# A Conformer block on one core: the small gate's halves trade partitions, small operations take their engine from a table, and the written-out orders are replaced

## The chip, the cores and the metric

The kernel runs on one core of one Trainium2 chip. Its time is the device time of one execution in microseconds, here the median of several runs. The core has four engines that compute, each with its own in-order queue: PE (matrix products into PSUM), ACT (activation functions, copies), DVE (elementwise work, statistics) and POOL (GpSimd, elementwise work without PSUM). SP's queue issues most DMAs. Engines wait for one another by semaphores. A queue never passes a waiting instruction, so the order in which instructions stand on an engine is part of the kernel.

## The reference

Two sequences of 4000 tokens, 144 channels, 4 heads of 36, a depthwise convolution of 5 taps; inputs and output are bf16.

```python
def reference(x, w_ff1a, w_ff1b, w_qkv, w_o, w_pw1, dw, w_pw2, w_ff2a, w_ff2b):
    h = _layernorm(x, axis=-1)
    h = _silu(h @ w_ff1a) @ w_ff1b
    x = x + 0.5 * h
    h = _layernorm(x, axis=-1)
    qkv = h @ w_qkv
    ...
    p = _softmax(scores, axis=-1)
    att = jnp.einsum('bhqk,bhkd->bhqd', p, v)
    ...
    x = x + att @ w_o
    h = _layernorm(x, axis=-1)
    h = h @ w_pw1
    a, b = (h[..., :D].copy(), h[..., D:].copy())
    h = a * _sigmoid(b)
    ...
    for i in range(K):
        c = c + hp[:, i:i + T, :] * dw[i][None, None, :]
    x = x + _silu(c) @ w_pw2
    h = _layernorm(x, axis=-1)
    h = _silu(h @ w_ff2a) @ w_ff2b
    x = x + 0.5 * h
    return _layernorm(x, axis=-1)
```

## The kernel before

The 8000 tokens are cut into 16 chunks of 500 (four blocks of 125 tokens), eight per sequence. Each chunk goes through the first feed-forward part and the projections (`pre`), then the attention of its 500 queries against the 4000 keys of its sequence, then what follows attention: the output projection (`post1`), the gated product (`glu`, `glu_left`), the convolution, the second feed-forward part and the last normalisation (`post2`). The parts before and after are spread between the tiles of attention of other chunks.

**Attention.** Keys come in tiles of 64, 62 per sequence and a rest of 32; 16 chunks times 63 give 1008 tiles in a fixed sequence. A tile takes four score matmuls (two heads at a time in two PSUM banks, 128x1000 values). For a tile of type A one ACT instruction takes the exponential of both banks into a slot of `PT`. For type D DVE makes it without ACT: two conversions of 128x500 to int16, a bit operation, a product and a second bit operation on 128x1000 (`ymw_args`); type W does both conversions in one instruction. R is the rest tile. A tile of type A needs four value matmuls, one of type D or W eight, since its exponential is a sum of two parts. Values gather in PSUM banks 6 and 7, and `epilogue` takes them out when a chunk is complete.

**The gated product.** Of the 144 channels, 128 go through `glu`. The other 16 of all four blocks are packed side by side by `glu_left`: the matmuls against the padded weights `WPZ` leave the value half in PSUM partitions 0 to 63 and the gate half in 64 to 127. ACT's tanh (the sigmoid is made from it) reads partitions 64 to 127 and writes `TH` on 0 to 63; a DVE instruction multiplies that with the value half. It runs once per chunk, 16 times.

**Small operations.** `copy` takes projections and transposes out of PSUM (`KT`, `QT`, `VA`, `XTB`, `XTQ`), on ACT or DVE. `residual` adds a product to `X`: ten or fewer matmuls for two blocks into one bank, then a DVE instruction that scales PSUM, adds `X` and writes `X`. `ln` makes a normalisation: statistics on DVE, then on one engine the variance plus epsilon (`RS` from `ST`), on POOL its reciprocal root (an exponent of -0.5), then the normalised rows `XN`, on POOL in the middle of the kernel, on DVE or ACT in the first chunks and at the end.

**What sets the order.** A planner runs the program once with costs and makes instructions in an order of its own, which also fixes what depends on what. Six tables then replace its choices. `TYPES` gives each tile its type; `BANKS` and `SLOTS` its PSUM banks and its slots of `PT`; `PLACES` the banks of all other PSUM tiles. `settle` builds the attention instructions anew from these. `ORDER` holds for each engine the order of all steps in two characters each; `Rec.arrange` sorts by it and derives the waits for PSUM banks and slots. `Rec.replay` then issues all instructions, so that most rows of the profile have its line, L546; instructions are told apart by the names of their tiles.

Of the kernel before, what the change touches and what calls it, by code (L numbers as in the profile page):

```python
# [13 lines left out]
H = 4  # L14
# [26 lines left out]
        '+V+U+?*z*{+4+I+<+O+M+N+Z+Y+2#-+^+_+1+P+F+b+E+c+D+3+C+J+f+m+l#.+p+q+W+e+d+X+u+t+`+]+g+[+n+o+x+y#/+}+|'
        '#0,,,+,$+a+v+T+S,0,/+w+s+z,!,%,4,3#1,8,7,.+r+j+k+{,1,B,A,<,;+Q+R,#+h,F,E,5,2,-,6,:,I,J+i,M,9,N,C,D#2'
        ',U,R,Q,(,&,*,),K,V,],[#3,`,a,S,P,=,@,d,e#4,h,i,T,l,G,H,>,?,r,s#5,v,w,L,O,m,j,z,{#6-#-!,k,f,b,c,g-&-.'
        '--#7-2-1,X,W,t-(,y,x-6-5-$-%,u-9,},|-:#8,Z-3-=->-4-7-A-8-F,Y-B-E-/-;-0-+-<-K-L-)-,-*-?-O-P-S-T,n-@,o'
        ',^-Z-Y,_-D,p,q-C-^-_#;#9-c-b#:#=#>#<-g-f-J-`-]-[-d-k-j-e-r-a-R-I-o-n#?#@-s-G-X-h-H-W-x-y#A#C#B-|-}-Q'
        '-z-l-i.%.$-{-M.--U-q.).*#D.3.4-N-p...!-m.7.8#E.;.<.@.+.(.5-V.?.##F.6.D.C.=.G-w.&.H.:.9.,-v-u.B.K.L.R'
        '.>.F.S.E.Y.X-t.J.2.].^./.O.0.e.N.M.b.a.I.t.f.1.A.Q.P#G#H.s.p.o.V.[.`.T.W.Z.d.i.x.w#I.u.h.g.j.|.{._.v'
        '.c.r.U.z.y/$/#/(///.#J/2/3/)/!/%/&.q/7/6#K/;/:#L.n/D/>/E/4/0/-/</1/H/=/I.}/?.m/5/8#M/M/L/,/9/*/Q/P/G'
        '#N/X/Y/O/N/F/+/B/K/U/T#O/_/S/i/h/l/C/p/m/J.l#P/q/R/A/Z/^/@/c/b/{/z/a/`/]0!0#/t/[/V.k/W0.0-#Q020&01/k'
        '060%0$050(/j/o0//}/u/|0@0?0409/s/n030D0C00#R0H0G/r08070:/f/g0K0L#S0P0O#T/d/e0S0T0A0E0F0_0M0N0^0B0+0,'  # L50
        '0W0)0g0c0b0R0I0J0Q0V0U0f0X#U0k0j0=0*0d0`0a0n0o#W0s0r0>#V#X0w0v0<0l0z0{0q0u0p0]/x0m0t0;/y1)1*0[0y0e1!'
        '1.1-#Y12110i1+0x1,0h1#1615#Z1:19#[1=1>#]1;1B1E1A1<17181%1$1(1K1&1L1F/w130|0}1O1P#^#_1S1T1@1?1C1X1I1N'
        '1D1Q1R1[1J1W1b1c1U0Z141M/v1]1/0Y1V1f1g#`1q1p1G1H1j101u1t#a1y1x1k1h1d1e1_1`2(2&1v1a1Z1|1^1i2,2+1{1z#b'
        '2/201Y1}2*1w2)292:231n1s2=2>1r#c211o2B2A2-242.2L2K2?2@1l2;2!2F2O2P2<1m2%2E2S2T#d2X2Q2W222M2N2#252R2U'
        '2]2[2$26#e282g2Z2C2`2V2a2h2Y#f2d2I2n2m2y2J2^2D2b2c2q2r2_2G2z2e2f2u2v2H273#3$#i#h3)3(2k2t3-3,#g30312w'
        '2x3&2}2l2o34352s3+2j3*3=3<39382i333!3%2p323B3C37363.3/3F3G#j3K3J2|3N2{3A3:3;3U3T3O3@3X3Y3M3D3a#k3^3]'
        '3E3L3>3h3S3g3Q3H3I3V3[3R3b3k3l3`3P#l3o3?3_3p3i3j3y3z3f3m3W3s3Z4!3n3}#m4&4%3q3t41403r4*4$3{3c3|4544#n'
        '49483d3e424+4#434=4<#o4@4A#p4E4D#q#r4H4I3w473x464L4M#t#s4V4W4/4.4,4)4(4K4[4Z#u4`4_4C4P4;4B4-4:4j4i4F'
        '4Q3u4G4d4n4m3v4b4c4a4Y4r4q4X4^4J4l4?4]4v4u#w#v5#4U4>5$4p5)4w4x4T4O5(4S4y4N4R4h5-5,4z4k#x51505+545&4s'
        '5.5/5:5;4e554g5*4f5?5>4o53524t5B5C5=5L#y5M4{5%5A4}4|5F5!5Q5P59565E5D#z5U5T5N5<575G5@5X5Y#{5^5]#|5b5a'  # L60
        '5S585W5V5f5Z5[5e5R5i5w5_5s5r5d5c5O5J5I5H5K5l5`5g5h5v5j5k5{5z#}5m6!6#5x5t5y6.6&$!6-5}6(5|6%616$62$#66'
        '65$$6364$%676:695u5p6>6/606=686+$&6H6G6A5q6<6K6L$(6B6I6O6*6P6@6)6Y6Z6?6;5o6S6N6,$)$*6M6_6]6^6c5n6b6J'
        '6E6R6Q6F6T6[$+6f6a6m6`6l6D6C6e6q6p6d6g$,6t6u$-6x6y$.6V6|7$6o6}6U6X6r$/7%7+7,6W6{6n706v6s6z6k7/736w7#'
        '796j7:7!$0746h7>7=7*7)6i717A7B$17E7F$27J7I7.7;$3727Q7N7M7-7($4757R7W7X7<7&767C7]7K7[7L78777@7f7P7?7H'
        '7O7g7`$57j7k7G7Z7U7a7Y7D7o7n$67y7x7i7^7_7h7r7T7}7|$77V8$8%7z7s7S7l7{8*8)$884838(8-7e7d8#8&8887$97q7p'
        '8!8.8;8<$:8?8@7b7m7t867u8C8>8I8J8=$;8M8N8+8D7v7c8K8,8Q8R898:8A8B$<8]8[7w8U8P85808/8a8`$=8e8d8V8S8_8O'
        '8H8G8c8h8i8b$>$?8m8l8g8f8p8T8^8L8j8k818z8y9!8}8o8E828s8F8n8X8W8Z8Y8q8r9&9%9+8t9*$@9.94958|9)989$9#8{'
        '99$A9=9<96979,9-9G8w9/9F9($B9K9J9>9;8x9@9O9N$C9S9R9:9A8u9I8v9W9V9L9?9M9H9Z9a9b$D9f9e9[909U92939T9j9i'
        '9Q$E9s9t9g9Y9h9P919m9x9w9d9c$F9|9{9n9C:*9X:+9B9z9^9u9v9`:#:/:.$G:29l9_:3:$:-9k:!9q9r:6:0:7:,9]9E:::1'
        ':A:@$H:4:;:8:E9y:D:(9p:):H9D9}:I:L9o:5:S:R$I:M:F:%:W:&:V:B:[:U:J:G:Z:_:?:9:C:e:f$J:=:<:j:i:`:X:Q:T:g'  # L70
        ':^:m:n:>:h:K:]:q:Y:w:x$K:{:|:r:o:P;#;$$L;/;.:a:O:y:d:p;2;3:c:N;6:z;(;7;!;0$M;1:}:t;@:s;A;E;:;&:u:v;D'
        ';%:k:l;);H;I;4:b;B;;;5;M;L$N$O;8;P;J;Q;U;N;,;O;9;T;F;C;+;*$P;_;G;X;`;-;K;>;c;S;=;d;R;Y;?;V$Q;h;g;<;W'
        ';l;k$R;w;o;p;e;f;i;j;^;];t;s$S;b;z;n;q;{<)<*<$;m<%$T$U<3<4;y;x<8<-<7<.;a;r;v;u;Z<<<;;[$V<?<@$W$X$Y$Z'
        '$[<C<D<,<5<H<&<(<9<:<+<G<2;|<0</<#<K<L<=<1;}<!<6<P<O<><S$]<Y<Z<T<I<F<E<_<^$^<J<b<h<i<A$_<l<m<]<`<B<M'
        '<Q<c<q<p$`<t<u<N<j$a<x<y<s<[<r=%<n<k<}<|<a=$<R<U<o=,=+<{<W<z<X=?<w=/=0<v<V$b=3=4$c$d$e$f=-=8=7=2=)=@'
        '=(=;=6=<=!=1=.<e=&<g<d=F=E=#=U<f=:=*=9=J=I$g=M=N=H===V=G=5=Q=R$h=]=[=P=O=l=D=>=K=a=`$i=d=e=m=S=B=L=A'
        '=i=h$j=s=r=^=c=C=Z=T=b=v=w$k=z={=u=Y$l=q>!>#=_=f=W=t=k>(>&=|$m>2>1=y=x>+=X=j=}>5>6$n>9>:>%>$>,=p=n=g'
        '>>>=$o>B>A>*>)$p>K>L>@>E>7>8=o>?>P>O$q>T>S>F>M>4>/><>;>X>W$r$s>[>]>.>Q>C>V>->0>f>R>3>D>`>g>H>Y>J>k>j'
        '$t>N>I>a>h>i>n>o>^>G>_>s>l>m>r>U>Z$u$v>v>p>w>d>q>z$w?!>b>u>t>}>c?%>e$x?,?->y>x>|>{?0?1?&?8?4?5?#?$?>'
        '??$y?C?B?9?.?/?3?F?G?J?@?7?A?6?P?Q$z?T?U?*?I?+?H?D?K?Y?X?E?R?]?S?)?2?d?c${?h?g?V?^?(?W?k?l$|?p?o?e?f'  # L80
        '$}?t?s?:?;?n?Z?w?j?m?[?}@!%!@%@&?i?x?M?q?<?r@1@0?_?=?u?O@#@+@4@5@*?`?v?L?N@8@9@$@2@<%#@B@C@=@F@G@7@3'
# [2306 lines left out]
```

## Time and profile before

| | |
|---|---|
| time, median of 3 runs | 878.67 us (878.53 to 880.87) |
| the profiled execution, its time | 879.67 us |
| its span on the core | 877.9 us |
| granted TensorE clock | 0.998 |
| exponentials on ACT, 128x1000 | 789 |
| tiles with the exponential on DVE (D and W) | 203 |
| small tanh of `glu_left`, 64x125 | 16 |

How to read the profile's rows: a row of grouped instructions has the line, the engine, the operation, output<-input by tile names, the shape and the count; behind the bar the busy time of the group in us and the mean duration of one in ns; then the idle time of the engine just before them and what ended it. In order of time, a row is the start, the duration in us, and the instructions merged into it. A row of a stretch has its length, then for each engine its busy time and its instructions, the granted clock, the DMA share and GB/s. A wait row names who waited for whom, the sum in us, how often, and the longest. PEld is PE's loading of weights, which runs ahead of the matmuls.

### The profile page before, as it was taken

What the parts mean: (1) busy time and instruction counts of PE and PEld (TensorE: products, weight loads), DVE (VectorE), ACT (ScalarE), POOL (GpSimd) and SP (SyncE); (2) the same over time, 40 slices, a digit from 0 to 9 for tenths busy, and PEclk for the clock granted to TensorE, in tenths of its full rate; (3) what the DMA queues carried; (4) which work ended last, traced back from release to release, by engine and by line L of the source; (5) the groups of instructions that cost most, each with busy time, mean ns of one, the idle gap of its engine ahead of it and who ended that gap; (6) DMA issues with size and microseconds to landing.
All of it is one profiled execution on the core that took longest, in us unless ns stands there. A gap on an engine that the chain in (4) does not pass through costs nothing.

```text
span 877.9 us, 26920 instructions
## 1 busy us (share of the span) xinstructions
PE 858.1 (98%) x11549; PEld 411.5 (47%) x11549; DVE 830.7 (95%) x1821; ACT 836.7 (95%) x1072; POOL 281.8 (32%) x544
## 2 busy tenths in 40 slices
PE   9999999999999999999999999999999999999996
PEld 7643534444444444434444444434435444444585
DVE  8999999999999999989999999999999999999887
ACT  6799989999999999999999999999999999999975
POOL 6570342311314303512230241122430453302734
PEclk9999999999999999999999999999999999999999
DMA  4520111211122111221120020100210122101201
GB/s 119 71 45 8 33 21 37 44 15 37 27 38 39 19 20 20 45 31 21 33 38 2 20 26 8 27 13 20 32 37 3 27 38 27 32 1 14 40 21 38
DMA packets 83551, 26.11 MB, mean 30 GB/s; under 512 B 78231, under 2 KB 83432, under 8 KB 83432
## 3 DMA queue, kind: packets, MB, share of 16 engines
q1 hardware_dynamic: 81884, 23.70, 15.5%
q8 instruction: 90, 1.47, 0.7%
q10 hardware_dynamic: 1548, 0.69, 0.3%
q14 instruction: 29, 0.24, 0.1%
HBM read 3.31 MB, written 2.30 MB: 6 GB/s over the span
## 4 chain that ended last, share of the span: by engine, by line
PE 45%; ACT 42%; DVE 9%; DMA 2%; POOL 1%; issue 1%; DVEq 0%
PE PS L546 45%; ACT PT L546 39%; DVE PT L546 5%; ACT TH L546 3%; DMA XTB<-XN 1%; DVE HT L546 1%; DVE ST L546 1%; DVE X L546 1%; DVE QT L546 1%; DMA X<-in_x_dram 0%; DVE KT L546 0%; DVE XN L546 0%; POOL RS L546 0%; POOL XN L546 0%; DVE RS L546 0%
## 5 line engine op out<-in xcount | busy, mean ns | idle before, releaser
L546 ACT ACTIVATE PT<-PS 128x1000 bf16<-128x1000 f32 (+1 forms) x805 | 743.0, 1086 | 7.9 <-PE PS L546 6.3
L546 PE MATMUL PS<-QT,KT 64*64 64x500 bf16 x3968 | 458.4, 384 | 6.9 <-ACT PT L546 1.7
L546 PE MATMUL PS<-PT,VA 64*37 64x500 bf16 x4780 | 447.2, 373 | 1.0 <-DVE QT L546 0.7
L546 DVE TENSOR_SCALAR PT<-PS 128x500 int16<-128x500 f32 x401 | 266.2, 678 | 11.8 <-PE PS L546 8.6
L546 PEld LDWEIGHTS PS<-QT,KT 64*64 64x64 bf16 x3968 | 139.7, 104 | 214.1 <-ACT PT L546 120.2
L546 PEld LDWEIGHTS PS<-PT,VA 64*37 64x37 bf16 x4780 | 161.1, 96 | 108.8 <-issue 21.0
L546 POOL TENSOR_SCALAR RS<-ST 125x4 f32<-125x4 f32 x118 | 34.7, 294 | 483.7 <-DVE ST L546 477.9
L546 DVE TENSOR_SCALAR PT<-PT 128x1000 uint16<-128x1000 uint16 x406 | 164.2, 418 | 3.1 <-PE PS L546 1.5
L546 DVE TENSOR_TENSOR PT<-PT 128x1000 bf16<-128x1000 bf16 x203 | 138.1, 682 | 1.7
L546 POOL TENSOR_SCALAR XN<-X,RS 125x144 bf16<-125x144 bf16 x236 | 129.0, 559 | 6.2
L546 POOL TENSOR_TENSOR RS<-RS,NHALF 125x4 f32<-125x4 f32 (+2 forms) x99 | 92.7, 939 | 41.5 <-DVE RS L546 36.2
L546 ACT ACTIVATE TH<-PS 128x500 bf16<-128x500 f32 (+3 forms) x175 | 97.9, 577 | 5.8 <-PE PS L546 3.9
L546 DVE SCALAR_TENSOR_TENSOR HT<-TH,PS 128x500 bf16<-128x500 bf16 (+1 forms) x120 | 72.2, 619 | 5.3 <-ACT TH L546 4.4
L546 PE MATMUL PS<-XTB,WA 72*128 72x500 bf16 (+2 forms) x304 | 72.1, 344 | 2.1 <-DMA XTB<-XN 1.7
L546 DVE BATCH_NORM_STATS2 ST<-X 125x6 f32<-125x288 bf16 (+1 forms) x160 | 66.2, 448 | 0.5 <-DMA X<-in_x_dram 0.4
L546 DVE SCALAR_TENSOR_TENSOR X<-PS,X 125x288 bf16<-125x288 f32 x128 | 57.3, 452 | 7.0 <-PE PS L546 6.3
L546 PE MATMUL PS<-WB,HT 128*125 128x144 bf16 (+1 forms) x640 | 51.9, 229 | 0.4 <-ACT HT L546 0.3
L546 PEld LDWEIGHTS PS<-WB,HT 128*125 128x125 bf16 (+1 forms) x640 | 44.6, 136 | 12.7 <-issue 5.0
L546 PEld LDWEIGHTS PS<-XTB,WA 72*128 72x128 bf16 x304 | 23.2, 97 | 28.3 <-issue 8.7
L546 POOL COPY U<-U 128x2 bf16<-128x2 bf16 (+1 forms) x54 | 12.8, 277 | 57.6 <-DVE U L546 43.0
L546 PE MATMUL PS<-U,DG 128*128 128x375 bf16 (+5 forms) x204 | 28.3, 263 | 0.0
L546 ACT ACTIVATE HT<-PS 128x500 bf16<-128x500 f32 (+3 forms) x46 | 21.7, 525 | 5.0 <-PE PS L546 4.5
(87 smaller groups left out, 518.6 us busy)
## 6 DMA issues: line engine op xcount, KB each, us to landing
X<-in_x_dram SPq DMA_DIRECT2D x16, 140.6 KB
XTQ<-XTB SPq DMA_DIRECT2D x24, 70.3 KB
out_dram<-XN SPq DMA_DIRECT2D x11, 140.6 KB
XTB<-XN SPq DMA_TRANSPOSE x50, 3.1
out_dram<-XN SPq DMA_DIRECT2D x6, 70.3 KB
XTB<-AN SPq DMA_TRANSPOSE x15, 3.4
out_dram<-XN ACTq DMA_DIRECT2D x3, 70.3 KB
WA<-in_w_ff1a_dram ACTq DMA_DIRECT2D x1, 144.0 KB
```

The source lines that it names most:

```text
L546: ins = getattr(eng, o.name)(*o.a, **o.k)
```

## The change

The tables `ORDER`, `PLACES`, `TYPES`, `BANKS` and `SLOTS` are replaced. `TYPES` now has 777 A, 209 D, 6 W and 16 R (before: 789, 198, 5 and 16). The two banks of a tile need not be neighbours any more, since the access patterns step from one to the other. A new table `UNITS` has a letter for each of 465 small operations, in the order in which the planner makes them: the engine that it runs on (a, d or p for ACT, DVE, POOL). `Rec.unit` registers such an operation with its alternatives and `Rec.choose` puts the chosen one in. Where a residual goes to ACT, PE adds `X` to the product by a matmul against an identity (`IDENT`, or `EYE` for scaled ones, made on POOL at the start), and ACT copies the sum to `X`. Where normalised rows change engine, the small instruction for the negated mean (POOL) or the scaled one (DVE) goes or comes with them.

In `glu_left` gate and value trade places: the padded weights are filled the other way round, the tanh reads PSUM partitions 0 to 63, and the product reads the value half from 64 to 127.

```diff
+    def choose(self, codes):
+        gone = set()
+        for code, (ops, own, alts, extras, ends, pre) in zip(codes, self.units):
+            if code == own:
+                continue
+            more = []
+            gone.update(id(o) for o in pre)
+            for eng, name, a, k, cost, kind, tile, deps in extras.get(code, ()):
...
+            for o, (eng, name, a, k, cost, lat) in zip(ops, alts[code]):
+                o.eng, o.name, o.a, o.k = eng, name, a, k
...
+    op("pool", "tensor_scalar", EYE[:, 0, :], IDENT[:, :], 2.0, None, op0=ALU.mult, r=["ID"], w=["EYE2"], cost=0.4)
+    op("pool", "tensor_scalar", EYE[:, 1, :], IDENT[:, :], 4.0, None, op0=ALU.mult, r=["ID"], w=["EYE4"], cost=0.4)
...
     def copy(dst, src, r, w, n, rate=1.0, eng=None, scale=1.0):
-        if (eng or flex()) == "act":
-            op("act", "activation", dst, src, ACT.Copy, bias=0.0, scale=scale, r=r, w=w, cost=c_act(n))
...
+        made = {"a": ("act", "activation", (dst, src, ACT.Copy), dict(bias=0.0, scale=scale), c_act(n), None)}
...
+        R.unit([o], code, {c: [v] for c, v in made.items()})
...
     def setup_dw():
         for ab in range(2):
-            op("dve", "tensor_copy", WPZ[0:HD, :, 48 + 64 * ab:64 + 64 * ab], WP1[0:HD, :, ab * D + ML:(ab + 1) * D],
+            op("dve", "tensor_copy", WPZ[0:HD, :, 112 - 64 * ab:128 - 64 * ab], WP1[0:HD, :, ab * D + ML:(ab + 1) * D],
...
     def residual(c, g, mm, scale, rk, e=False):
...
+        R.unit([o], "d", {"a": [("act", "activation", (xv(c, bs, rows), ps, ACT.Copy), dict(bias=0.0, scale=scale),
+                                 c_act(2 * D), None)]},
+               {"a": [("pe", "matmul", (PSV[0:rows, bk, i * D:(i + 1) * D],), dict(
+                   lhsT=eye[0:rows, 0:rows], rhs=X[0:rows, c * NB + b, :], start=False, stop=True, skip_group_check=True), 0.0645, "f", ends[0].tile, deps)
+                      for i, b in enumerate(bs)]}, ends)
...
     def glu_left(c, s):
...
-        op("act", "activation", TH[0:64, t, 0:TB], PSV[64:128, bk, 0:TB], ACT.Tanh, bias=0.0, scale=0.5,
-           r=[("ps", bk), "TAB0"], w=[("TH", t)], cost=c_act(TB) + 0.28)
+        o = op("act", "activation", TH[0:64, t, 0:TB], PSV[0:64, bk, 0:TB], ACT.Tanh, bias=0.0, scale=0.5,
+           r=[("ps", bk), "TAB0"], w=[("TH", t)], cost=c_act(TB) + LEFT)
+        R.trims.append((o, LEFT))
         yield need("dve", hold=True)
         op("dve", "scalar_tensor_tensor", out=U2[0:64, u, 1:1 + TB], in0=TH[0:64, t, 0:TB], scalar=1.0,
-           in1=PSV[0:64, bk, 0:TB], op0=ALU.add, op1=ALU.mult, r=[("TH", t), ("ps", bk), "U20"], w=[("V", u)],
+           in1=PSV[64:128, bk, 0:TB], op0=ALU.add, op1=ALU.mult, r=[("TH", t), ("ps", bk), "U20"], w=[("V", u)],
            cost=c_dve(TB))
...
-        return (PT[:, pt, :, :], PSV[:, lo:hi + 1, 0:CH], ACT.Exp), k
+        return (PT[:, pt, :, :], PSV[:, lo:hi + 1:hi - lo, 0:CH], ACT.Exp), k
...
     def settle():
+        R.choose(UNITS)
```

Counted in the built instruction order of both kernels: ACT has 12 exponentials less and, more than before, 16 residual evictions, 10 copies of 128x500 into `KT` and `QT`, 3 copies into `VA` and 10 normalisations of one block; it has 2 copies less into each of `XTB` and `XTQ`. DVE has 12 more tiles of five (W: four) instructions. PE has 48 more value matmuls and 32 identity matmuls. 12 two-block variance operations move from DVE to POOL and 15 four-block ones the other way; POOL has six two-block negated means more and three four-block ones less, since 12 blocks of normalised rows come to it and 12 leave it.

More of the change, by code (lines that the diff above doesn't have):

```diff
@@ L41 @@
[L41 to L45, printed above, removed]
@@ L394, in op, with unit @@
         return o
+    def unit(self, ops, code, alts, extras=None, ends=(), pre=()):
+        self.units.append((ops, code, alts, extras or {}, ends, pre))
+    def choose(self, codes):
[6 more added lines that the diff above has]
+            for eng, name, a, k, cost, kind, tile, deps in extras.get(code, ()):
+                o = Op()
+                o.eng, o.name, o.a, o.k, o.q, o.kind, o.quads, o.att = eng, name, a, k, None, kind, (), None
+                o.deps = list(deps) + [(d, True) for d, raw in ops[0].deps if raw]
+                o.inc, o.cnt, o.tile, o.shared, o.own, o.step = False, 0, tile, set(ops[0].shared), set(ops[0].own), ops[0].step
+                o.t0, o.t1, o.done = 0.0, cost, cost + self.LAT[eng]
+                more.append(o)
+            if any(o.eng == "pe" for o in more):
+                for o in ends:
+                    o.k["stop"] = False
+            for o, (eng, name, a, k, cost, lat) in zip(ops, alts[code]):
+                o.eng, o.name, o.a, o.k = eng, name, a, k
+                o.t1 = o.t0 + cost
+                o.done = o.t1 + (self.LAT[eng] if lat is None else lat)
+                o.deps = o.deps + [(x, True) for x in more]
+            self.ops = more + self.ops
+        self.ops = [o for o in self.ops if id(o) not in gone]
+        for o in self.ops:
+            o.deps = [d for d in o.deps if id(d[0]) not in gone]
+            o.shared, o.own = o.shared - gone, o.own - gone
     def ready(self, key, eng):
@@ L1200, in ln @@
         else:
+            code = "d"
             yield need("dve")
-            for j in range(n):
-                op("dve", "tensor_scalar", xn(u, j), xi(j), ST[0:rows, u, j, 1:2],
-                   RS[0:rows, u, 0, j:j + 1], op0=ALU.subtract, op1=ALU.mult,
-                   r=[("X", c, b0 + j), ("MV", u), ("RS", u)] + xe, w=[("XN", u)], cost=0.231)
+        pre = []
+        if code in signs:
+            g = signs.pop(code)
+            pre = [op(g[0], g[1], *g[2], **g[3], r=[("MV", u)] + [("RS", u)] * (code == "a"), w=[("NM", u)], cost=g[4])]
+            if code == "a":
+                yield need("act")
+            R.step += 1
@@ L1206, in ln @@
+        alts.pop(code)
+        deps = [(d, True) for key in (("MV", u), ("RS", u)) for d in R.history(key)[0]]
+        R.unit(ops, code, alts, {q: [g[:7] + (deps,)] for q, g in signs.items()}, pre=pre)
+        R.step += 1
         return u
```

551 lines of the change are left out of this document (299 added, 252 removed).

## The prediction

> **What bounds the kernel now.** I read the page's busy shares first, then the busy time of each engine in five stretches, cut where the exponentials of key tiles 124 and 945 start, where the last exponential ends, and at the first one.
>
> ```profile
> span 877.9 us, 26920 instructions
> PE 858.1 (98%) x11549; PEld 411.5 (47%) x11549; DVE 830.7 (95%) x1821; ACT 836.7 (95%) x1072; POOL 281.8 (32%) x544
> ...
> core 0: us, PE busy (x) PEld busy (x) DVE busy (x) ACT busy (x) POOL busy (x), PEclk, DMA share, GB/s
> 0.00:19.40 19.40, 17.66 (x200) 15.25 (x201) 16.20 (x62) 10.74 (x23) 13.18 (x32) 1.00 0.45 119
> 19.40:146.00 126.60, 124.09 (x1660) 58.47 (x1656) 122.61 (x275) 116.70 (x152) 50.42 (x91) 1.00 0.22 40
> 146.00:782.00 636.00, 627.83 (x8568) 280.33 (x8568) 607.12 (x1248) 630.91 (x774) 179.00 (x353) 1.00 0.15 26
> 782.00:830.40 48.40, 48.14 (x668) 22.77 (x660) 46.18 (x98) 48.11 (x60) 19.09 (x34) 1.00 0.11 17
> 830.40:878.00 47.60, 40.40 (x474) 34.67 (x466) 38.57 (x142) 30.21 (x67) 20.11 (x35) 0.96 0.16 36
> ```
>
> The mean hides three regimes. In the middle, 636 us long, ACT is busy 630.9: 5.1 us are left. DVE has 28.9 left there. In the front (19 to 146) it is DVE that is full, 122.6 of 126.6, while ACT has 9.9 free. After 830 no engine but PE is near full; that stretch is a chain of dependences.
>
> PE's 98% is no bound: its ends are modelled. The waits of the middle stretch say so:
>
> ```profile
> PEld PS L546 <- ACT PT L546: 107.3, 321, 0.8
> ...
> DVE PT L546 <- PE PS L546: 9.5, 24, 0.7
> ...
> ACT PT L546 <- PE PS L546: 2.9, 7, 0.6
> ACT TH L546 <- PE PS L546: 0.8, 2, 0.5
> ```
>
> PE's weight loads waited 107.3 us for an exponential to free a score bank; ACT waited 3.7 us (2.9 + 0.8) for PE. So PE follows ACT. What the change does to ACT's load in the middle decides most, and how much of DVE's 28.9 us it uses up comes next.
>
> **The change part by part.** The counts come from the built instruction order of both kernels, engine by engine.
>
> *1. The gate's swap.* Its small tanh reads PSUM partitions 64 to 127 and writes 0 to 63, 16 times, 14 of them in the middle. ACT in order of time, around one of these and around another small tanh (80x125, no crossing):
>
> ```profile
> 265.04 1.01 ACT L546 ACTIVATE PT<-PS 128x1000 bf16<-128x1000 f32 x1
> 266.08 0.28 ACT L546 ACTIVATE TH<-PS 64x125 bf16<-64x125 f32 x1
> 266.38 2.79 ACT L546 ACTIVATE PT<-PS 128x1000 bf16<-128x1000 f32 x3
> ...
> 489.59 0.76 ACT L546 ACTIVATE TH<-PS 128x500 bf16<-128x500 f32 x1
> 490.06 0.78 ACT L546 ACTIVATE PT<-PS 128x500 bf16<-128x500 f32 x1
> 490.53 0.31 ACT L546 ACTIVATE TH<-PS 80x125 bf16<-80x125 f32 x1
> 490.68 2.87 ACT L546 ACTIVATE PT<-PS 128x1000 bf16<-128x1000 f32 x3
> ...
> 588.18 26.00 ACT PT L546 x29
> ```
>
> Neighbours on ACT normally overlap: the 500-wide one lasts 0.76 but the next starts 0.47 later, and 29 exponentials in a row take 26.00, 0.897 each. The crossing tanh starts only after the exponential has ended (265.04 + 1.01 = 266.05) and the next starts after it has ended. From exponential to exponential that is 1.34 us, so the tanh costs 1.34 - 0.897 = 0.44; the 80x125 one costs 490.68 - 490.53 = 0.15. The swap saves 0.29 each, **4.1 us** of ACT in the middle (14 x 0.29). The other two lie in the last stretch, where ACT has slack.
>
> The crossing moves to the DVE product, which now reads the value half from partitions 64 to 127. DVE in order of time:
>
> ```profile
> 266.63 0.27 DVE L546 SCALAR_TENSOR_TENSOR U<-TH,PS 64x125 bf16<-64x125 bf16 x1
> 266.83 0.73 DVE L546 TENSOR_SCALAR PT<-PT 128x1000 uint16<-128x1000 uint16 x2
> 267.48 0.67 DVE L546 TENSOR_SCALAR PT<-PS 128x500 int16<-128x500 f32 x1
> 268.07 0.66 DVE L546 TENSOR_TENSOR PT<-PT 128x1000 bf16<-128x1000 bf16 x1
> 268.66 0.66 DVE L546 SCALAR_TENSOR_TENSOR U<-TH,PS 128x500 bf16<-128x500 bf16 x1
> ```
>
> No row shows a crossing on DVE. Bounds: nothing, or ACT's 0.29, the only crossing in the trace. I take 0.29: 4.1 us of DVE in the middle. The Trainium skill, page "VectorE: DVE Perf Modes", section "Two Vector instructions with no wait between them", speaks against this half of the change: a Vector instruction whose input starts in another quadrant than the last read of that memory is held until all earlier ones have finished. By that rule the product and the next reader of PSUM each lose the overlap seen above (0.27 long, next one 0.20 later, so 0.07), an estimate of 0.14 each and 2.0 us in place of 4.1; no run here shows it yet.
>
> *2. Key tiles.* The type table moves 12 of 1008 tiles from ACT's exponential to the DVE one, 11 in the middle. Each takes 0.897 off ACT: **-9.9 us**. On DVE a tile is two conversions (267.48 to 268.07, 0.59 each), one product (268.07 to 268.66, 0.59) and two bit operations (266.83 to 267.48 for two, 0.33 each): 2.43, so +26.7 us.
>
> *3. Small operations.* In the middle ACT receives four 500-wide Q or K copies, two 504-wide and one 72-wide V copies and nine residual evictions of 288 columns. In the front:
>
> ```profile
> 15.66 0.38 ACT L546 ACTIVATE KT<-PS 128x250 bf16<-128x250 f32 x1
> 15.94 0.37 ACT L546 ACTIVATE QT<-PS 128x250 bf16<-128x250 f32 x1
> 16.23 0.58 ACT L546 ACTIVATE XTQ<-PS 72x500 bf16<-72x500 bf16 x1
> ...
> 12.37 0.46 DVE L546 SCALAR_TENSOR_TENSOR X<-PS,X 125x288 bf16<-125x288 f32 x1
> 12.74 0.54 DVE L546 TENSOR_SCALAR XN<-X,ST,RS 125x144 bf16<-125x144 bf16 x2
> 13.19 0.45 DVE L546 BATCH_NORM_STATS2 ST<-X 125x6 f32<-125x288 bf16 x1
> ```
>
> A 250-wide copy takes ACT 0.28 (15.66 to 15.94), a 500-wide 0.47; for 288 columns I take 0.31. ACT: 6 x 0.47 + 0.1 + 9 x 0.31 = **+5.7 us**. DVE is relieved of six at 0.59, nine residuals at 0.37 (12.37 to 12.74) and about 0.1: -7.0; nine variance operations come from GpSimd at under 0.1: +0.7.
>
> PE gains the residual sums: 32 identity matmuls in all, and 44 matmuls for the 11 tiles in the middle.
>
> ```profile
> L546 PE MATMUL PS<-PT,VA 64*37 64x500 bf16 x4780 | 447.2, 373 | 1.0 <-DVE QT L546 0.7
> L546 PE MATMUL PS<-WO,XTB 72*125 72x144 bf16 x128 | 13.7, 235 | 0.0
> ```
>
> At 447.2/4780 = 0.094 and 13.7/128 = 0.107 that is 4.1 + 3.4 us, hidden under the 107.3 us that PE waits for ACT; without that cover it would cost the 7.5.
>
> *Sum of the middle.* ACT: -9.9 - 4.1 + 5.7 = -8.3, to 622.6 us. DVE: 607.1 + 26.7 - 7.0 + 0.7 + 4.1 = 631.6. If ACT stays the bound with its 5.1 us idle, the stage takes 627.7. But then DVE would have to be busy longer than the stage. It can only be met because DVE's busy time holds tails: an instruction of 0.67 is followed 0.59 later when the next is ready, and the 0.08 counts as busy when it isn't. The 170 products of this stage alone:
>
> ```profile
> L546 DVE TENSOR_TENSOR PT<-PT 128x1000 bf16<-128x1000 bf16 x170 | 115.6, 682 | 1.5
> ...
> 734.00:782.00 48.00, 47.37 (x634) 20.99 (x628) 47.07 (x97) 47.48 (x59) 12.02 (x25) 1.00 0.14 21
> ```
>
> They are busy 115.6 but need 170 x 0.59 = 100.3 back to back. All 1248 instructions have 1248 x 0.08 = 100 us of tails, part of them already covered. The last 48 us of the stage show both engines full at once: DVE 47.07, ACT 47.48. The middle therefore lies between -8.3 (ACT decides) and +7.8 (DVE keeps the idle share of that window, 0.93/48 = 1.9%: 631.6/0.981 = 643.8). ACT is the engine with no idle time to give and this window shows DVE keeping up with it, so I place the stage near ACT's end and give 2.3 us back for tails that stay: **-6**.
>
> *Front, to 146 us.* ACT receives six 500-wide Q or K copies, two residuals, four normalisations, one V copy less and net one transpose copy less: about +3.7 us on 9.9 us of slack. DVE, the full one, loses six at 0.59, two at 0.37 and four normalisations at 0.23 (12.74 to 13.19 for two), and gets a V copy and a transpose copy back: -4.4. The normalisations on ACT have no row; the nearest is the 250-wide 0.28, 1.1 for four. By the Trainium skill, page "ScalarE: Activation LUTs", section "What ACT_TABLE_LOAD costs", each pointer operand adds some 93 ns; a normalisation has two, so by that page the four cost an estimated 0.7 us more; no row of this run has such an instruction. GpSimd gets two scaled identities at its start and a new order:
>
> ```profile
> 9.22 1.50 POOL L546 TENSOR_TENSOR RS<-RS,NHALF 125x2 f32<-125x2 f32 x2 [2.15 <-DVE RS L546]
> 10.67 0.55 POOL L546 COPY WQ<-WQKV 72x144 bf16<-72x144 bf16 x2
> 11.16 0.55 POOL L546 COPY WK<-WQKV 72x144 bf16<-72x144 bf16 x2
> ```
>
> The third reciprocal root, at 9.22 now, will stand behind these weight copies, which take 10.67 to 11.71, 1.0 us: whoever normalises next waits so much longer. So between -4.4 and +1; I take **-2.5**, a little over half of DVE's relief, since ACT's 9.9 us of slack shrink by 3.7 at the same time.
>
> *From 782 us on.* One tile more on DVE (+2.4), five residuals (-1.9) and six normalisations (-1.4) less, three transpose copies back (+1.0); ACT about 0. Only the order differs: 0, give or take 1.
>
> Sum: -6 - 2.5 + 0 = -8.5: span 869.4. The profiled execution took 879.67, 1.8 more than its span, and the median of the runs shown is 878.67; from there **870.2 us**.
>
> **Rivals.** *DVE takes over and eats the gain.* The middle keeps its 636 us, the front's 2.5 remain: 876.2, between 874.5 and 878. For it: 24.5 us more work on an engine with 28.9 idle. Against it: the 48 us window.
>
> *Slower: the DVE queue.* The five instructions of each added tile wait for one another on an in-order engine; everything behind them (residuals, PSUM evictions) waits too, and PE for their banks. From 4.4 us of DVE idle in the middle (636 - 631.6) the stage is longer than now, from 6.9 the front's 2.5 is gone too; at 1.9% idle (12.2 us) it is +7.8 and the total 878.67 + 7.8 - 2.5 = 884.0. For it: the busy sum above. Against it: ACT has had the bound so far, so DVE never had to close its gaps.
>
> *The swap does nothing.* If the gaps around the small tanh come from something else than the crossing, ACT keeps 4.1 us: 874.3. Against it: the 80x125 tanh shows none.
>
> *The front loses.* If the later root holds up the first chunk by 1 us and nothing is gained: 878.67 - 6 + 1 = 873.7.
>
> **How the numbers follow.** Forecast 0.57 (its own range 864 to 874), DVE level 0.18, DVE slower 0.13, swap idle 0.04, front 0.08. About 0.3% (2.6 us) can be told from no change. Below 876.0 lie the forecast, the swap, the front and 0.08 of the DVE-level case: faster 0.77; the rest of that case is same, 0.10; slower 0.13. Everything good at once gives 878.67 - 8.3 - 4.4 - 1 = 865.0, and the low end leaves 2 us below it for what the new order closes in gaps; the upper end takes in DVE level and part of the slower case: 863 to 880.
>
> **What would show it.** Around the 64x125 tanh the neighbours overlap and it costs some 0.15. ACT busy over the middle falls by 8, at 99% still. DVE rises above 97% there; waits of ACT for PE stay below 10 us. If ACT shows idle time of 10 us or more in the middle while DVE is at 98%, the DVE rivals are right. The first exponential, now just behind the 19.4 cut, tells of the root; tile 124, now at the 146 cut, should start near 143.5. Wrong would be a middle no shorter, or a gain that comes from behind 830.

## The result, and the profile after

The changed kernel takes 882.11 us in the median of 17 runs (881.10 to 886.16), the kernel before 878.67: ratio 1.0036, 95% interval 1.0024 to 1.0047. It is 0.4% slower, where 870.2 was forecast. Ratios, here and below, compare with runs of the kernel before on the same chip, and can differ a little from the quotient of two medians.

The page of the changed kernel: span, busy shares, and the granted clock in 40 slices.

```profile
span 881.0 us, 27134 instructions
PE 859.1 (98%) x11629; PEld 417.4 (47%) x11629; DVE 845.8 (96%) x1853; ACT 837.7 (95%) x1095; POOL 284.7 (32%) x546
...
PEclk7999999999999999999999999999999999999999
```

The first slice has a 7. The stretches, cut at the same events as before (just ahead of the first exponential, of tile 124, of tile 945, and at the last exponential's end), columns as before:

```profile
0.00:26.50 26.50, 21.66 (x201) 19.01 (x201) 16.39 (x57) 11.62 (x25) 13.91 (x35) 0.81 0.43 124
26.50:151.40 124.90, 122.98 (x1660) 58.35 (x1657) 119.98 (x267) 119.98 (x161) 51.92 (x96) 1.00 0.18 32
151.40:784.10 632.70, 625.35 (x8630) 281.71 (x8631) 622.34 (x1295) 625.82 (x779) 180.26 (x344) 1.00 0.15 26
784.10:832.50 48.40, 48.27 (x680) 23.28 (x676) 47.22 (x103) 48.04 (x62) 13.75 (x23) 1.00 0.08 16
832.50:881.00 48.50, 40.82 (x482) 35.09 (x470) 39.89 (x135) 32.24 (x72) 24.81 (x50) 0.96 0.16 36
```

Against before: the start +7.1 (19.4 to 26.5), the rest of the front -1.7 (126.6 to 124.9), the middle -3.3 (636.0 to 632.7), the last tiles 0.0, the tail +1.0 (47.5 to 48.5). That makes the +3.1 of the span. The change gains 5.0 in the front and the middle; it loses more than that ahead of the first exponential, with the granted clock at 0.81.

The waits of the middle (151.4 to 784.1 us) of the changed kernel: who waited for whom, sum, times, longest.

```profile
PEld PS L591 <- ACT PT L591: 88.8, 278, 0.7
...
ACT PT L591 <- PE PS L591: 3.8, 13, 1.0
...
DVE PT L591 <- PE PS L591: 1.4, 6, 0.4
...
ACT X L591 <- PE PS L591: 0.8, 2, 0.5
...
ACT TH L591 <- PE PS L591: 0.8, 3, 0.4
```

DVE hardly waits for PE any more (9.5 to 1.4), and PE waits 18.5 us less for ACT.

**What happens at the start.** POOL and DVE of the changed kernel in order of time:

```profile
5.89 1.40 POOL L591 TENSOR_TENSOR RS<-RS,NHALF 125x2 f32<-125x2 f32 x2 [3.17 <-DVE RS L591]
7.25 0.58 POOL L591 MEMSET WP2Z<- 128x576 bf16 x1
...
9.25 0.52 POOL L591 MEMSET WK<- 128x512 bf16 x1
...
10.21 0.54 POOL L591 COPY WK<-WQKV 72x144 bf16<-72x144 bf16 x2
```

```profile
6.66 4.19 DVE L591 TENSOR_SCALAR XN<-X,ST,RS 125x144 bf16<-125x144 bf16 x4 [0.28 <-POOL RS L591]
```

And the same two engines in the kernel before:

```profile
1.46 0.58 POOL L546 MEMSET WP2Z<- 128x576 bf16 x1
...
3.46 0.52 POOL L546 MEMSET WK<- 128x512 bf16 x1
5.69 1.38 POOL L546 TENSOR_TENSOR RS<-RS,NHALF 125x2 f32<-125x2 f32 x2 [1.71 <-DVE RS L546]
```

```profile
1.52 2.53 DVE L546 CAST IDF<-IDENT 128x128 f32<-128x128 bf16 x1
...
6.44 1.22 DVE L546 TENSOR_SCALAR XN<-X,ST,RS 125x144 bf16<-125x144 bf16 x4 [0.26 <-POOL RS L546]
```

Before, POOL cleared seven tiles between 1.46 and 3.98, while the first X was still on its way. The new order puts these memsets, and the weight copies behind them, after the first two reciprocal roots: 7.25 to 10.75. That is when DVE normalises the first chunk. Four rows that took 1.22 now take 4.19, and they stand still, they don't wait: a stalled row counts as busy. The same sign stood in the profile of before, unread: a small cast of 2.53 us beside the same memsets.

PE, which needs the rows, stands idle for 3.06 us and has 0.68 us of work in the 4 from 7 to 11, and then its clock is halved. The end of the wait and three stretches of the changed kernel:

```profile
10.90 0.63 PE L591 MATMUL PS<-IDENT,XN 125*72 125x125 bf16 x4 [3.06 <-DVE XN L591]
```

```profile
7.00:11.00 4.00, 0.68 (x8) 0.51 (x9) 3.87 (x4) 0.00 (x0) 3.75 (x12) 0.90 0.34 118
11.00:15.00 4.00, 4.00 (x25) 3.13 (x26) 2.03 (x10) 2.03 (x4) 2.04 (x3) 0.50 0.62 164
15.00:21.00 6.00, 6.00 (x55) 5.77 (x54) 2.52 (x11) 2.93 (x5) 1.38 (x2) 0.54 0.50 138
```

### The profile page after: what moved, and what is told of

It reads as the page before. It is cut to its first block, busy times and chain, and to the rows that moved or that the text cites. A ratio compares the mean times of both kernels' runs of the same rounds, so it can differ in the third digit from the quotient of the medians.

```text
span 881.0 us, 27134 instructions
## 1 busy us (share of the span) xinstructions
PE 859.1 (98%) x11629; PEld 417.4 (47%) x11629; DVE 845.8 (96%) x1853; ACT 837.7 (95%) x1095; POOL 284.7 (32%) x546
## 4 chain that ended last, share of the span: by engine, by line
PE 41%; ACT 38%; DVE 17%; DMA 2%; issue 1%; POOL 1%; DVEq 0%; POOLq 0%; ACTq 0%
PE PS L591 41%; ACT PT L591 34%; DVE PT L591 11%; ACT TH L591 3%; DVE ST L591 1%; DMA XTB<-XN 1%; DVE XN L591 1%; DVE X L591 1%; DVE U L591 1%; DMA X<-in_x_dram 0%; DVE QT L591 0%; DVE HT L591 0%; DVE KT L591 0%; POOL RS L591 0%; DVE SW L591 0%
## 5 line engine op out<-in xcount | busy, mean ns | idle before, releaser
L591 ACT ACTIVATE PT<-PS 128x1000 bf16<-128x1000 f32 (+1 forms) x793 | 731.8, 1075 | 6.6 <-PE PS L591 5.2
L591 PE MATMUL PS<-PT,VA 64*37 64x500 bf16 x4828 | 452.0, 373 | 1.8 <-DVE QT L591 0.9
L591 DVE TENSOR_SCALAR PT<-PS 128x500 int16<-128x500 f32 (+1 forms) x424 | 280.4, 679 | 4.7 <-PE PS L591 2.7
L591 POOL TENSOR_SCALAR RS<-ST 125x4 f32<-125x4 f32 (+1 forms) x118 | 31.1, 264 | 485.6 <-DVE ST L591 481.2
L591 DVE TENSOR_SCALAR PT<-PT 128x1000 uint16<-128x1000 uint16 x430 | 172.0, 417 | 1.7 <-PE PS L591 0.5
L591 DVE TENSOR_TENSOR PT<-PT 128x1000 bf16<-128x1000 bf16 x215 | 145.8, 681 | 1.1
L591 POOL TENSOR_SCALAR XN<-X,RS 125x144 bf16<-125x144 bf16 x236 | 134.4, 581 | 4.0 <-DMA out_dram<-XN 0.3
L591 POOL TENSOR_TENSOR RS<-RS,NHALF 125x4 f32<-125x4 f32 (+2 forms) x99 | 97.0, 983 | 75.2 <-DVE RS L591 73.0
L591 DVE SCALAR_TENSOR_TENSOR X<-PS,X 125x288 bf16<-125x288 f32 (+1 forms) x112 | 50.1, 451 | 8.6 <-PE PS L591 7.6
L591 ACT ACTIVATE HT<-PS 128x500 bf16<-128x500 f32 (+3 forms) x46 | 21.7, 523 | 5.4 <-PE PS L591 5.0
L591 DVE TENSOR_SCALAR XN<-X,ST,RS 125x144 bf16<-125x144 bf16 (+1 forms) x74 | 23.1, 421 | 0.5 <-POOL RS L591 0.3
```

The source lines that it names most:

```text
L591: ins = getattr(eng, o.name)(*o.a, **o.k)
```

## The experiments

The table gathers them. Starts of exponentials are from each profiled execution, in us; the middle runs from tile 124's exponential to tile 945's. The groups a, b, c and d ran on four chips, on which the kernel before took 878.66, 879.83, 879.71 and 878.92 us: medians compare within a letter, ratios between letters.

| kernel | median us | ratio to before [95%] | first exp. | tile 16 | middle |
|---|---|---|---|---|---|
| before | 878.67 | 1 | 19.6 | 56.5 | 636.3 |
| after | 882.11 | 1.0036 [1.0024, 1.0047] | 26.7 | 62.6 | 633.1 |
| a1 memsets first | 879.77 | 1.0001 [0.9985, 1.0016] | 19.2 | 60.2 | 632.9 |
| a2 identities, memsets first | 878.70 | 1.0009 [0.9993, 1.0024] | 19.1 | 57.0 | 633.5 |
| a3 before, memsets late | 883.11 | 1.0050 [1.0037, 1.0064] | 24.3 | 60.3 | 635.1 |
| a4 after, PE filled | 875.94 | 0.9967 [0.9954, 0.9979] | 22.2 | 58.1 | 631.9 |
| b1 before, swap | 879.76 | 0.9991 [0.9974, 1.0009] | 19.6 | 56.8 | 636.6 |
| b2 as a1, no swap | 882.07 | 1.0022 [0.9996, 1.0049] | 18.9 | 64.0 | 634.5 |
| c1 as a2, loads late | 875.68 | 0.9948 [0.9934, 0.9963] | 19.0 | 55.0 | 632.6 |
| c2 as c1, no swap | 875.80 | 0.9953 [0.9936, 0.9969] | 19.3 | 55.3 | 633.9 |
| c3 before, loads late | 878.48 | 0.9976 [0.9964, 0.9989] | 19.5 | 55.6 | 636.2 |
| c4 as c3, swap | 878.31 | 0.9976 [0.9962, 0.9990] | 19.5 | 55.6 | 636.1 |
| d1 as c1, no crossing | 874.56 | 0.9953 [0.9937, 0.9970] | 18.9 | 54.8 | 632.1 |
| d2 as c1, both cross | 876.44 | 0.9972 [0.9953, 0.9991] | 18.9 | 54.8 | 635.6 |

### a1 and a2: POOL's memsets back in front

The order string holds two characters a step: `!$` are the memsets, `!#` the scaled identities, `!%` and `!&` the first roots, `!(` the weight copies. a1, then a2:

```diff
-        '!!!#!%!&!$!(!)!-!*!+ ...
+        '!!!$!%!&!(!#!)!-!*!+ ...
```
```diff
-        '!!!#!%!&!$!(!)!-!*!+ ...
+        '!!!#!$!%!&!(!)!-!*!+ ...
```

> The changed kernel with POOL's start put back: the large memsets stand ahead of the first reciprocal root, the two scaled identities behind the weight copies. Theory (collision): while POOL fills memory, DVE's first normalised rows stand still, and the gap that this leaves on PE halves its granted clock. Then the four rows take 1.2 us again instead of 4.19, the granted clock stays at 1.0 in the first 20 us, the first exponential starts near 19.5 instead of 26.5, and the time is 882.1 - 7 = 875 us (874 to 876.5). Rival (the new order of DVE and ACT in the first chunk is to blame): the first exponential stays behind 24 us and the time above 880.

> As the run with the memsets first, but the two scaled identities (1.17 us of POOL) stand at the very start, ahead of the memsets. Theory (collision): POOL is done near 5.2 us, before the first statistics ask for a root at 5.9, so the time is that of the other run within 0.5 us. Rival (the scaled identities delay the first root): the first root starts about 1 us later and so does the first exponential.

The collision is gone in both: the first exponential starts at 19.2 and 19.1. The scaled identities at POOL's start delay nothing. But the time doesn't come back in full: a1 was expected at 874 to 876.5 and took 879.77, and a2 lies 1.1 us from it and not within 0.5. a1's 12 runs lie between 876.6 and 882.0, and in its profiled execution tile 16 is 3.7 us late again. There is a second place, between 19 and 60 us. Stretches of a1 and its waits from 18 to 60 us:

```profile
24.00:27.00 3.00, 3.00 (x42) 2.13 (x36) 2.79 (x8) 2.72 (x4) 2.07 (x3) 1.00 1.63 152
27.00:30.00 3.00, 1.37 (x7) 0.50 (x6) 2.95 (x6) 1.90 (x4) 2.87 (x8) 1.00 0.41 99
30.00:35.00 5.00, 5.00 (x24) 1.93 (x26) 2.46 (x6) 2.70 (x6) 4.81 (x11) 0.65 0.28 52
```

```profile
PEld PS L591 <- DMA XTB<-XN: 2.1, 1, 2.1
...
PE PS L591 <- DMA XTB<-XN: 1.6, 1, 1.6
```

PE waits for rows that a DMA transposes (`XTB` from `XN`), and its clock falls, to 0.65 on the mean of these 5 us. In a2's profiled execution PE has a like gap (1.21 us of work from 27 to 30), but the clock stays at 1.00, and tile 16 starts at 57.0. SP's queue of a1 shows what that DMA met:

```profile
16.78 4.47 SPq L591 DMA_DIRECT2D X<-in_x_dram  x8
23.46 13.65 SPq L591 DMA_TRANSPOSE XTB<-XN  x3
```

Eight loads of later chunks of X are still landing (the DMA share of 24 to 27 us is 1.63, against 0.34 in the changed kernel) when the first transpose is issued. In the changed kernel, seven us late, the first transpose is issued at 30.99, and the loads were through by then. So the early start runs into something that the late one avoids.

### a3: the kernel before with its memsets moved late

```diff
             lines[e] = [o for i in at for o in blocks[keys[i]]]
+        line = lines["pool"]
+        lines["pool"] = line[:3] + line[10:12] + line[3:10] + line[12:]
```

> The kernel before with one edit: the seven large memsets of POOL stand behind the first two reciprocal roots. Theory (collision): the first four normalised rows take 3 to 4 us instead of 1.22, PE idles about 3 us, its granted clock falls to 0.5 for some microseconds, the first exponential comes 5 to 7 us later, and the time is 884 to 886. Rival (the tables of the change are to blame): less than 1.5 us over the time of the kernel before.

One move of seven memsets reproduces the loss in the kernel before: 1.0050, with the first exponential 4.7 us later. Both are a little less than expected (884 to 886, and 5 to 7 us). The four rows and the clock of a3:

```profile
6.01 3.21 DVE L548 TENSOR_SCALAR XN<-X,ST,RS 125x144 bf16<-125x144 bf16 x4 [0.26 <-POOL RS L548]
```
```profile
7.00:11.00 4.00, 1.92 (x18) 1.47 (x16) 3.46 (x7) 0.58 (x1) 2.33 (x8) 0.82 0.37 125
11.00:15.00 4.00, 4.00 (x25) 3.18 (x23) 1.33 (x6) 3.05 (x7) 2.16 (x6) 0.50 0.61 166
```

### a4: the changed kernel with PE's gap filled

56 matmuls against the identity, whose result nobody reads, stand between the first two groups of transposes; nothing else is changed.

```diff
+        line, fill = lines["pe"], []
+        for _ in range(56):
+            o, w = Op(), line[54]
...
+            fill.append(o)
+        lines["pe"] = line[:57] + fill + line[57:]
+        self.ops = self.ops + fill
```

> The changed kernel with 56 more identity matmuls, whose result nobody reads, in PE's gap between the first two groups of transposes. DVE still stands still for about 3 us. Theory (the gap costs twice, by the wait and by the clock): the granted clock stays at 1.0 from 11 to 21 us, the first exponential comes near 23 and the time is 882.1 - 3.5 = 878.6 (877.5 to 879.5). Rival (the whole delay is DVE's): no change, 881 to 883.

```profile
6.54 4.18 DVE L599 TENSOR_SCALAR XN<-X,ST,RS 125x144 bf16<-125x144 bf16 x4 [0.28 <-POOL RS L599]
```
```profile
7.00:11.00 4.00, 3.87 (x67) 3.76 (x68) 3.87 (x5) 0.00 (x0) 3.63 (x12) 1.00 0.37 123
11.00:15.00 4.00, 4.00 (x53) 3.70 (x51) 2.64 (x12) 3.63 (x8) 2.04 (x3) 1.00 0.59 163
```

The rows stand still as long as ever, but the clock stays at 1.00 and the first exponential comes at 22.2 instead of 26.7. So of the 7.1 us the stall itself is 2.6 and the halved clock 4.5; against a2, the same tables without the stall (19.1), they are about 3 and 4.5. With nothing taken out, 56 useless matmuls make the changed kernel faster than before: 0.9967. At 875.94 it is also faster than expected (877.5 to 879.5).

### b1 and b2: the swap by itself

b1 is the kernel before with the three lines of the gate swap; b2 is a1 with them undone.

```diff
-        op("act", "activation", TH[0:64, t, 0:TB], PSV[64:128, bk, 0:TB], ACT.Tanh, bias=0.0, scale=0.5,
+        op("act", "activation", TH[0:64, t, 0:TB], PSV[0:64, bk, 0:TB], ACT.Tanh, bias=0.0, scale=0.5,
...
```

> The kernel before with the swap of the gate's halves alone; tables and orders stay. Theory (ACT is the bound of the middle and takes what it is given): 0.29 us less on ACT for each of 14 small tanh there, the stage 3 to 4 us shorter, the time 875 to 876. Rival (the order was made for the crossing, and PE's and DVE's instructions stand where they stood, so that ACT waits for scores instead): 0 to 1.5 us less. Both: the small tanh loses its gaps of 24 ns on either side; the DVE product takes 0.12 us longer from end to end, and so does the next instruction that reads PSUM.

> The changed kernel with the memsets first and the swap undone (crossing on ACT again). Theory (ACT still bounds the middle): 3 to 4 us over the run with the memsets first. Rival (DVE now bounds the middle, and it gets the crossing off its back): 0 to 1.5 us over it, or less time.

On the old orders the swap gives nothing that can be told from 0 (0.9991, interval around 1), as the rival had it. b2 tells little: its runs lie between 877 and 888, because the place of a1 strikes harder (tile 16 at 64.0, the clock at 0.50 to 0.57 from 30 to 45 us).

### c1 to c4: loads out of the transposes' way, with and without the swap, on new and old orders

Six of the eight late loads of X go behind the first three transposes on SP.

```diff
+        line = lines["sp"]
+        lines["sp"] = line[:23] + line[29:32] + line[23:29] + line[32:]
```

> The changed kernel with GpSimd's start mended (identity pieces, the seven memsets, then the first roots), and six of the eight late X loads (the chunks first read after 70 us or later) issued behind the first three DMA transposes instead of in front of them. Theory A (what an early start still loses is lost because the first DMA transposes are issued at 23.4 us into loads that run until 27 us: the transposed rows land late, TensorE stands still and its clock falls): DMA share of 24 to 27 us falls from 1.57 to under 0.6, TensorE's waits for the transposed rows from 2 to 4 us to under 1, granted clock 1.00 throughout 18 to 60 us, first exponential at 18.9, last exponential at 825 to 827, time 872 to 875, and the runs of it lie within 1 us of each other. Theory B (the loads have nothing to do with it; the new orders of 19 to 60 us simply start with more work in front): the share falls, but tile 16 still starts 0.5 to 4 us later than before and the time stays at 877 to 880 with a spread of some us.

> The same as the run before it, with the gate swap undone (the tanh reads rows 64 to 127 again). If the new orders and tables use what the swap gives ScalarE (14 crossings of 0.29 us: up to 4 us), this is 3 to 4 us slower than its twin: 876 to 878. If the swap is worth as little there as it was on the old orders, it is within 1 us of its twin.

> The kernel before with the six late X loads behind the first three DMA transposes and nothing else. Theory A: it loses 1.6 us to the first transposed rows as it stands, so it gains 1 to 2 us: 876.5 to 878, with a smaller spread. Theory B: no change, 878.7.

> The run before it with the gate swap added. If the swap alone is worth what it takes from ScalarE's path, 3 to 4 us below its twin (873 to 874.5); if ScalarE on the old orders only waits for something else instead, within 1 us of its twin.

c1 in the same stretches as a1:

```profile
24.00:27.00 3.00, 3.00 (x36) 2.11 (x33) 2.79 (x7) 2.72 (x4) 2.18 (x3) 1.00 0.46 87
27.00:30.00 3.00, 3.00 (x18) 1.54 (x16) 3.00 (x7) 2.74 (x7) 2.90 (x7) 1.00 0.00 0
30.00:35.00 5.00, 5.00 (x55) 2.85 (x54) 4.78 (x10) 4.75 (x11) 4.81 (x11) 1.00 0.57 57
```

Theory A holds in its mechanism: the wait for the transposed rows is gone, the clock stays at 1.00, tile 16 starts at 55.0, and the six runs lie within 1.5 us (1 was expected). The last exponential ends at 824.7, 5.9 earlier than before. c1 is the fastest of the study that computes everything, 0.9948 of before, and with the ratio of the changed kernel 0.9948/1.0036 = 0.9912 of that: the places of some memsets and loads, which cost the bound engines nothing by themselves, were worth 6 to 8 us (882.11 - 875.68 by the medians, 0.0088 x 882 by the ratios). Of the forecast of c1, 872 to 875, the median 875.68 misses by a little. The kernel before gains from the late loads too (c3, 0.9976), as its own wait for the first transposed rows said.

The four together separate the rest. The new orders and tables are worth 2.7 us (c3 to c2, 878.48 to 875.80; 2.0 by the ratios), and in the middle 2.3 (636.2 to 633.9). The swap is worth 0.2 on the old orders and 0.1 on the new, where one of the theories had 3 to 4; in the traces' middle it is 0.1 and 1.3 (b2 to a1: 1.5). The five traces of the new orders with the swap (after, a1, a2, a4, c1) differ by 1.6 there, so 1.3 stands at the edge of what one trace can tell.

### d1 and d2: the two prices of the swap

Both are c1; d1 lets neither engine read across partitions, d2 lets both.

```diff
-           in1=PSV[64:128, bk, 0:TB], op0=ALU.add, op1=ALU.mult, r=[("TH", t), ("ps", bk), "U20"], w=[("V", u)],
+           in1=PSV[0:64, bk, 0:TB], op0=ALU.add, op1=ALU.mult, r=[("TH", t), ("ps", bk), "U20"], w=[("V", u)],
```
```diff
-        o = op("act", "activation", TH[0:64, t, 0:TB], PSV[0:64, bk, 0:TB], ACT.Tanh, bias=0.0, scale=0.5,
+        o = op("act", "activation", TH[0:64, t, 0:TB], PSV[64:128, bk, 0:TB], ACT.Tanh, bias=0.0, scale=0.5,
```

> The run with the late loads and the gate swap (c1, 875.68, 0.9948 of before) with the value read from rows 0 to 63 as well, so that neither ScalarE's tanh nor VectorE's product takes its 64 rows across partitions; the product is then formed of the gate's own input and not of the value. Theory A (both prices lie on the path and cancel in the swap: 16 crossings of 0.2 us on ScalarE, 3.3, against 16 products with 0.12 more on VectorE, 1.9, or whatever makes them equal): 1.9 us or more below c1 and its unswapped twin, so 0.9925 to 0.993 of before, 873.5 to 874. Theory B (the middle goes by the ring of TensorE and its two readers, and a saving of some tenths of a microsecond on one of them every 40 us is made up for by a wait for TensorE): within 1 us of c1, 0.994 to 0.996.

> The same with both readers crossing (tanh and product both read rows 64 to 127, the product then of the value's own gate). Theory A: 3.3 us above c1 and 5 above d1, 0.998 to 0.999 of before. Theory B: within 1 us of c1 and d1.

Theory B holds for d1: 0.9953 lies in its range, and by the ratios d1 is no faster than c1 (0.9948) and c2 (0.9953). That its median is 1.1 us below c1's says less, since the two ran on different chips. d2 lies between the theories (0.9972). It is 1.9 us above d1 (876.44 - 874.56), where A said 5 and B under 1, and their intervals overlap. Its middle of 635.6 is not the price of the crossings: in the profiled execution PE waited 1.0 us at 429 us for rows that a DMA copies, and from 432 to 435 the granted clock was 0.58. Up to 429 us d2 runs within 0.1 us of c2, counted from tile 124. So no crossing is shown to cost time at the end; by the ratios a single one, on ACT or on DVE, is worth 0.5 us or less in all 16 products, which these runs can't tell from 0.

## Why the prediction was wrong

Of the 11.6 us between the forecast span, 869.4, and the measured 881.0, 7.9 lie in the front, 2.7 in the middle and 1.0 behind 782.

**The step that failed** is the start order of GpSimd in the front's term, "will stand behind these weight copies, which take 10.67 to 11.71, 1.0 us: whoever normalises next waits so much longer", priced at 1.0 us at most for one root. The prediction counted how long POOL's own queue would be later, and only the weight copies in it. It missed that seven memsets were moved as well, onto DVE's first normalisation, what a memset does to DVE, and what a gap of PE does to its clock. The front's term of -2.5 became +5.4 (+7.1 - 1.7). The -1.7 behind the first exponential is the part that the step did count; without the collisions it is -1.5 (c3 to c1, 126.4 to 124.9 from there to tile 124). The root that the step named was not held up by the copies. They end at 10.75, and POOL then waits 1.87 us for DVE's statistics:

```profile
12.62 2.04 POOL L591 TENSOR_TENSOR RS<-RS,NHALF 125x2 f32<-125x2 f32 x3 [1.87 <-DVE RS L591]
```

a1, a2 and a3 show the cause from both sides, a4 splits it. The rival "the front loses" had the place right and its price at 1 us. The rival that came nearest in time, DVE's queue at 884.0, did so by luck: it has the middle 7.8 us longer, and the middle got shorter.

The Trainium skill, page "SBUF — State Buffer", section "Who interferes with whom", has a rule that fits the stall: DVE in its two-port mode and GpSimd share one pair of ports, and the later of the two blocks until the earlier instruction is finished. The trace agrees in kind, though no row shows the mode that DVE ran in: the longest of the four instructions lasted 3473 ns, the shortest 314,

```profile
L591 DVE TENSOR_SCALAR XN<-X,ST,RS x4: 314/1800/3473, 6.7 to 7.6; 125x144 bf16<-125x144 bf16 x4
```

but in size it waited out POOL's whole row of memsets and copies, 7.25 to 10.75, and not the 0.58 of the memset that was running. The Trainium skill, page "TensorE: Matmul & The Clock Gate", section "Part 1: The HAM clock gate", gives half the clock after an idle window of about 3.4 us and the full one after a busy window as long. Both differ here. Shorter gaps of PE were enough for the fall, 3.06 us in the changed kernel, 2.08 in a3 and 1.63 in a1, while a2's of 1.79 had none. The recovery took longer: the clock is 0.50 from 11 to 15 and 0.54 from 15 to 21 us, with PE busy all the time.

**The middle** was forecast at -6 and came at -3.3. Its parts:

- *Load of ACT.* It fell by 5.1 (630.9 to 625.8), not 8.3, and stayed at 99% (625.82/632.70). Counted from one start to the next, the small operations that came to it took 6.8 and not 5.7 (a residual 0.36 and not 0.31, a 500-wide copy 0.59 and not 0.47), and the swap took about 2.7 off its busy time and not 4.1. DVE took 622.3 and not 631.6, at 98.4%, above 97% as forecast: the 11 tiles that came to it cost 21.7 and not 26.7, since more of its tails were covered. The rivals built on DVE fell, since the middle got shorter and ACT's idle time there is 6.9 us (632.7 - 625.8), under the 10 of their sign. But DVE's share of the chain that ended last rose from 9% to 17%.
- *The swap.* The mechanism is as told. ACT around the small tanh in the changed kernel, then DVE around the product:

```profile
263.85 2.85 ACT L591 ACTIVATE PT<-PS 128x1000 bf16<-128x1000 f32 x3
266.52 0.27 ACT L591 ACTIVATE TH<-PS 64x125 bf16<-64x125 f32 x1
266.72 2.87 ACT L591 ACTIVATE PT<-PS 128x1000 bf16<-128x1000 f32 x3
```
```profile
266.30 0.68 DVE L591 TENSOR_SCALAR PT<-PS 128x500 int16<-128x500 f32 x1
267.01 0.29 DVE L591 SCALAR_TENSOR_TENSOR U<-TH,PS 64x125 bf16<-64x125 bf16 x1
267.33 0.68 DVE L591 TENSOR_SCALAR PT<-PS 128x500 int16<-128x500 f32 x1
```

The neighbours overlap, and the tanh costs 266.72 - 263.85 - 3 x 0.897 = 0.18 where it cost 0.44. On DVE the product and the conversion behind it start only when what is ahead has ended: 267.33 - 266.30 = 1.03 against 0.59 + 0.20 without a crossing, 0.24 more in all, below the 0.29 taken. That is the rule of the Trainium skill, page "VectorE: DVE Perf Modes", section "Two Vector instructions with no wait between them": the trace agrees that both are held, but the prediction's estimate by it, 0.14 for the two together, was too low. What failed is the step from ACT's load to the time, "So PE follows ACT". It was read from one line of a view that has this one too (the kernel before, 146 to 782 us):

```profile
PEld PS L546 <- DVE PT L546: 47.3, 151, 0.6
```

PE follows both engines. Its waits, 150 to 750 us, in c2 and in c1:

```profile
PEld PS L593 <- ACT PT L593: 91.9, 281, 0.7
...
PEld PS L593 <- DVE PT L593: 51.4, 171, 0.7
```
```profile
PEld PS L593 <- ACT PT L593: 82.7, 259, 0.7
...
PEld PS L593 <- DVE PT L593: 55.9, 184, 0.9
```

With the swap PE waits 9.2 us less for ACT and 4.5 more for DVE. The old orders show the same exchange (c3 to c4: 100.1 to 93.7 for ACT, 42.3 to 47.3 for DVE), although DVE is only 95% busy there and 98% on the new ones. PE's banks are emptied by both engines in a fixed order, and relief for one is answered by a wait for the other. In c4 the small tanh overlaps the exponential ahead of it as intended, but behind six of the 14 in the middle ACT then stands idle for 0.06 to 0.48 us. The rival "the swap does nothing" had the swap's worth right, though not its reason, since the gaps do come from the crossing.

- *Tiles and small operations.* Forecast -9.9 + 5.7 = -4.2 on ACT, and with the measured 6.8 it is -3.1; the orders and tables without the swap are worth 2.3 in the middle (c3 to c2).

**Normalisations on ACT**, of which the kernel before has none, were taken at 0.28 each, and the Trainium skill, page "ScalarE: Activation LUTs", section "What ACT_TABLE_LOAD costs", was cited for some 93 ns more for each of two pointer operands. Two in a row in the changed kernel:

```profile
40.19 0.91 ACT L591 ACTIVATE XN<-X,RS 125x144 bf16<-125x144 bf16 x2
40.99 1.83 ACT L591 ACTIVATE TH<-PS 128x500 bf16<-128x500 f32 x4
```

0.80 for two, 0.40 each: 0.12 above what was taken, so the page's direction holds and the four cost 0.5 more. **From 782 on** 0 was forecast, give or take 1, and +1.0 came, all of it in the tail. Its cause stays open: behind the last exponential the other runs with the new orders take 47.0 (c2) to 48.5 us (a2), those with the old ones 47.3. What the prediction named as signs told the truth: tile 124 started at 151.6 and not near 143.5, and the first exponential "tells of the root", 7.1 us late.

## What to carry to other kernels

Setup work that is "free" on a slow engine has a place: look at which rows of other engines run beside it, and at rows whose duration is many times that of their like, since a stalled instruction counts as busy. A gap in front of PE costs more than its length when the clock falls after it, and a few useless matmuls in the gap can be a cheap mend. And a saving on the fullest engine need not come out in the time, even where the next engine has room (DVE at 95% on the old orders): look at what else the engines around it wait for, and undo the one edit on both orders before crediting it.

## What the hardware showed that was not expected

- Memsets of POOL held up a 125x144 operation of DVE for 3.5 us instead of 0.3, until POOL's whole unbroken row was through; a 128x128 cast took 2.53 us beside them.
- The granted clock fell to 0.50 after gaps of PE of 3.1 us (the changed kernel), 2.5 (b2), 2.1 (a3) and 1.6 (a1), and not after one of 1.8 (a2). Once it had fallen it stayed down for some 10 us in the changed kernel, 7 in a1 and a3 and 14 in b2, with PE busy nearly all the time.
- A DMA transpose issued into loads that are still landing took up to 2.7 us to issue in a1, where c1's took 1.2 to 1.4, and PE stood idle for 1.6 us until its rows came. With six loads moved behind it, the spread of the runs went from 6.5 us in a2 (877.2 to 883.6) to 1.5 in c1 (874.6 to 876.2). It was 5.1 in d1 and 6.5 in d2, which issue them as c1 does, so the loads are not its only source.
- A late start can hide such a collision: from 24 to 27 us the changed kernel (7 us late) and a4 (3 us late) have a DMA share of 0.34, a1 has 1.63.
